# Query transposes moved to a block's end, a prologue with its own PSUM layout, and early steps shifted, in a pooled attention followed by a maxout FFN

The kernel runs on one core of one Trainium2 chip. The metric is the device time of that core in microseconds (us), lower is better. "Span" is the time from the first to the last instruction of the one execution that was profiled; it is about 1.8 us shorter than the measured time of that execution (231.8 beside 233.62 for the kernel before).

## What is computed

```python
# q, k, v: (8 batches, 8 heads, 576 tokens, 64)
k_p = k.reshape(B, H, 72, 8, 64).mean(axis=3)          # keys and values pooled by 8
v_p = v.reshape(B, H, 72, 8, 64).mean(axis=3)
attn = softmax(q @ k_p.T / 8)
x = (attn @ v_p) as 4608 tokens x 512                  # heads side by side
h = max(x @ w1, x @ w2, x @ w3)                        # 512 -> 768
out = h @ w_out                                        # 768 -> 512
```

The kernel uses h = x·w1 + max(0, x·(w2−w1), x·(w3−w1)). The product w1·w_out is made once (`linear`, result `wm`), so only two of the three wide products are done per token.

## The kernel before

Work goes in nine blocks of 512 tokens. Each block has "hidden" parts (x times a weight, then relu and maximum) and "project" parts (the output). A plan says which attention steps of the next batch are slipped in ahead of which part: `k` turns the pooled keys, `T` transposes the queries by DMA, `q` does that on TensorE, `s` makes scores, `v` values, `x` transposes an attention chunk into xT, `d` subtracts w1 from a third of w2 and w3, `w` transposes a piece of w1. A capital `K`, `Q` or `X` is the same step done or copied on VectorE. The number in a pair is the batch.

```python
pools = [stage.enter_context(tc.tile_pool(name="psp", bufs=1, space=PSUM))]
ATT, SC, TR, PW = ("att", 2), ("sc", 2), ("tr", 1), ("pw", 3)   # PSUM tags, buffers

def load_q(b):                                   # GpSimd issues the loads
    qbs[b] = ld.tile([128, 4, NG, D], BF16, name="qb", tag="qb")    # ld: two buffers
    ...
def sub_w(i):
    part = slice(256 * i, 256 * i + 256)
    for t in w_sb[1:]:
        nc.vector.tensor_tensor(out=t[:, :, part], in0=t[:, :, part],
                                in1=w_sb[0][:, :, part], op=ALU.subtract)
...
# ---- end of the prologue, batch 0 (psc: two buffers of two banks) ----
scores2(0)
xn0 = [values(0, c0) for c0, _ in CHUNKS[:2]]
heat(1)                                          # a warming matmul
turn_x(0, 0, 0, xn0[0], PW)
scores2(2)
turn_w(0, nc.scalar.copy)
turn_x(0, 128, 0, xn0[1], PW, nc.vector.tensor_copy)
sub_w(0)
scores2(4)
turn_w(1, nc.vector.tensor_copy)
scores2(6)
nc.vector.memset(kz_all[1], 0.0)

block(0, {0: [(0, "v2")], 1: [(0, "v3 d1")], 2: [(0, "x2")], 3: [(0, "x3 w2")],
          4: [(0, "v4")], 6: [(0, "x4")], 8: [(0, "w3")], 9: [(0, "d2")], ...
          32: [(1, "v1 x0")], 33: [(1, "X1 v2")]}, (hidden, project))

def plan1():                                     # block 1
    return {0: [(1, "v3")], 1: [(1, "x2")], ..., 6: [(2, "k")], 8: [(2, "q0")],
            9: [(2, "q1")], ..., 24: [(2, "x4")], 17: [(2, "s6"), (3, "T")]}

def plan(n):                                     # blocks 2 to 4
    b = n + 1
    ...
    got[1] = [(b + 1, "T")]

# pool_work(n, mm), in words: at the start of block n, all on GpSimd:
#   load k, v, q of batch n + 3, in this order, if there is one,
#   then fold the keys and values of the batches that FOLDS_OF names
```

Chunks of batches 3 and up are also transposed into xT by DMA, from the same queue (SP) as the output stores.

The softmax here doesn't subtract the row's maximum and nothing guards it: scores larger than these inputs give would overflow.

Of the kernel before, what the change touches and what calls it, by code (L numbers as in the profile page):

```python
# [14 lines left out]
def kernel(  # L15
# [11 lines left out]
    nc = tc.nc  # L27
# [3 lines left out]
    B, H, S, D = q.shape  # L31
# [16 lines left out]
    NB = 512  # L48
# [8 lines left out]
    ctx.enter_context(stage)  # L57
    pools = [stage.enter_context(tc.tile_pool(name="psp", bufs=1, space=PSUM))]

# [123 lines left out]
    def turn_k(b):  # L183
        pkt = keys(b, ATT if len(pools) == 1 else SC)
        for par, evac in enumerate((nc.vector.tensor_copy, nc.scalar.copy)):
            fill_kz(b, par, 0, H, pkt, evac if b > 2 else nc.vector.tensor_copy)
# [50 lines left out]
    def values(b, c0):  # L237
        tag = ATT if len(pools) == 1 else ("val", 1)
        pav = psum([128, 2, 512], F32, name="pav", tag=tag[0], bufs=tag[1])
        for h in range(H):  # L240
            nc.tensor.matmul(  # L241
                pav[:, h // 4, 65 * (h % 4):65 * (h % 4) + 65],
                ets[b][:, h, c0:c0 + 128], vp_all[:, b, h, :],
                start=True, stop=True)
        pv = pav[:, :, 0:260].rearrange("p g (h e) -> p g h e", e=65)
        rcp = sb3.tile([128, 2, 4], F32, name="rcp", tag="rcp")
        nc.vector.reciprocal(out=rcp, in_=pv[:, :, :, 64])  # L247
        xn = sb3.tile([128, 2, 4, D], F16, name="xn", tag="xn", bufs=6)
        nc.vector.tensor_tensor(  # L249
            out=xn, in0=pv[:, :, :, 0:D],  # L250
            in1=rcp.to_broadcast([128, 2, 4, D]), op=ALU.mult)
        return xn

    CHUNKS = ((0, 0), (128, 0), (256, 0), (384, 0), (448, 64))
    ATT = ("att", 2)
    SC = ("sc", 2)
    TR = ("tr", 1)
# [5 lines left out]
    def do(b, steps):  # L263
# [3 lines left out]
        for name in steps.split():  # L267
# [4 lines left out]
            elif name[0] == "T":  # L272
                qTs[b] = sb2.tile([128, 2 * NG, 128], BF16, name="qT", tag="qT")
                nc.sync.dma_start_transpose(
                    out=qTs[b], in_=qbs[b].rearrange("p hp t d -> p (hp t d)"))
            elif name[0] == "k":
                turn_k(b)
            elif name[0] == "K":
                fold_k(b, nc.vector)
            elif name[0] == "p":  # L280
                pool_v(b, 4 * i, 4 * i + 4, TR, nc.scalar.copy)
            elif name[0] == "s":
                if i == 0:
                    new_et(b)
                (scores if len(pools) == 1 else scores_flat)(b, i)
            elif name[0] == "d":
                sub_w(i)
            elif name[0] == "w":
                turn_w(i, nc.scalar.copy if i % 2 else nc.vector.tensor_copy)
            elif name[0] == "v":  # L290
                xns[b, i] = values(b, CHUNKS[i][0])
            else:
                turn_x(b, *CHUNKS[i], xns[b, i], ATT if len(pools) == 1 else SC,
                       nc.vector.tensor_copy if name[0] == "X" else nc.scalar.copy)
# [3 lines left out]

    def sub_w(i):

        part = slice(256 * i, 256 * i + 256)
        for t in w_sb[1:]:
            nc.vector.tensor_tensor(out=t[:, :, part], in0=t[:, :, part],  # L303
# [43 lines left out]
    def hidden(n):  # L347
# [3 lines left out]
        if halves:  # L351
            for c0 in (0, NB // 2):
                for jc in range(3):
                    yield from hidden_part(n, jc, c0, c0 + NB // 2, hT)
        for jc in range(3 if halves else 0, JCH):
# [4 lines left out]
    def project(n):  # L360
        hT = hTs[n]
        for mm in range(4):
# [3 lines left out]
            for c in ((slice(0, C // 2), slice(C // 2, C)) if last else (slice(0, C),)):  # L366
                tag = PW if len(pools) == 1 else (PO, SC, PA)[max(0, m - (TOK // 128 - 7))]
                po = psum([128, c.stop - c.start], F32, name="po", tag=tag[0], bufs=tag[1])
# [18 lines left out]

    wm = psum([128, 512], F32, name="wm", tag="tr", bufs=1)

# [6 lines left out]
    k16 = const.tile([96, 6, 4, D], F16, name="k16", tag="k16")  # L396
    pkp0 = psum([128, 6, D], F32, name="pkp", tag="pw", bufs=3)
    heat(10)
# [22 lines left out]
    put_k0(4, 6)  # L421
    turn_q(0, 0, 5, nc.vector.tensor_copy, PW)
    turn_q(0, 5, 9, nc.scalar.copy, ATT)
    pkt0 = [keys(0, PW) for _ in range(2)]
    for h in (0, 4):
# [3 lines left out]
    def scores4(h):  # L429
        psc = psum([128, 4, 256], F32, name="psc4", tag="att", bufs=2)  # L430
        for i in range(4):
# [3 lines left out]
    def scores2(h):  # L435
        psc = psum([128, 2, 512], F32, name="psc2", tag="att", bufs=2)
        for i in range(2):
# [4 lines left out]
    scores4(0)  # L442
    turn_q(0, 9, 14, nc.vector.tensor_copy, PW)
    turn_q(0, 14, 18, nc.vector.tensor_copy, PW)
    pool_v(0, 0, 4, PW, nc.vector.tensor_copy)
    scores4(4)
    pool_v(0, 4, 6, PW, nc.vector.tensor_copy)
    pool_v(0, 6, 8, PW, nc.vector.tensor_copy)
    scores2(0)
    xn0 = [values(0, c0) for c0, _ in CHUNKS[:2]]  # L450
    heat(1)
    turn_x(0, 0, 0, xn0[0], PW)
    scores2(2)
    turn_w(0, nc.scalar.copy)
    turn_x(0, 128, 0, xn0[1], PW, nc.vector.tensor_copy)
    sub_w(0)
    scores2(4)
    turn_w(1, nc.vector.tensor_copy)
    scores2(6)


    nc.vector.memset(kz_all[1], 0.0)
    xns[0, 0], xns[0, 1] = xn0

    FOLDS = (3, 4, 5, 6, 7, 8, 9, 11)

    def block(n, plan, parts, folds=()):

        for slot, _ in enumerate(part for stage in parts for part in stage(n)):
# [5 lines left out]
            if folds and slot in FOLDS:  # L475
                next(folds.pop(0))

    fold_v(1)
    block(0, {0: [(0, "v2")], 1: [(0, "v3 d1")], 2: [(0, "x2")],
              3: [(0, "x3 w2")], 4: [(0, "v4")], 6: [(0, "x4")],  # L480
              8: [(0, "w3")], 9: [(0, "d2")], 12: [(0, "w4")], 13: [(0, "w5")],
              17: [(1, "K")], 24: [(1, "q0 k")], 25: [(1, "q1")],
              26: [(1, "s0 q2")], 27: [(1, "s1 s2")], 28: [(1, "s3 Q3")],
              29: [(1, "s4 s5")], 30: [(1, "s6 s7")], 31: [(1, "v0")],
              32: [(1, "v1 x0")], 33: [(1, "X1 v2")]}, (hidden, project))
    load_k(3, nc.gpsimd)
# [6 lines left out]
    def plan1():  # L493
        return {0: [(1, "v3")], 1: [(1, "x2")], 2: [(1, "v4")], 3: [(1, "x3")],
                5: [(1, "x4")],
                6: [(2, "k")], 8: [(2, "q0")], 9: [(2, "q1")], 11: [(2, "q2 s0")],
                12: [(2, "s1 q3")], 13: [(2, "s2")], 14: [(2, "s3")], 15: [(2, "s4")],
                16: [(2, "s5")], 18: [(2, "s7")],
                19: [(2, "v0")],
                20: [(2, "v1 x0")], 21: [(2, "v2 x1")], 22: [(2, "v3 x2")],  # L500
                23: [(2, "v4 x3")], 24: [(2, "x4")], 17: [(2, "s6"), (3, "T")]}

    def plan(n):
# [3 lines left out]
        got.update({12 + c: [(b, f"v{c} x{c}")] for c in range(5)})  # L507
        got[1] = [(b + 1, "T")]
        return got
# [3 lines left out]
    def pool_work(n, mm):  # L513
# [5 lines left out]
        for name in FOLDS_OF.get(n, "").split():  # L519
# [11 lines left out]

    LEAD = {0: [(6, "s0")], 1: [(6, "s1"), (7, "T")], 2: [(6, "s2")], 3: [(6, "s3")],
            4: [(6, "s4")], 5: [(6, "s5")], 6: [(6, "s6")], 7: [(6, "s7")],
# [277 lines left out]
```

## Time and profile before

| | kernel before |
|---|---|
| three timed runs | 233.75, 235.48, 238.98 us (median 235.48) |
| profiled execution | 233.62 us, span 231.8, granted TensorE clock 0.997 |
| TensorE busy | 221.3 us, 95% |
| VectorE, ScalarE, GpSimd busy | 55%, 52%, 60% |

The page and the chain that the prediction shows carry most of the argument: TensorE is 90% busy or more in every slice from the fifth (23.2 us on) to the 39th. (The prediction says from the sixth; the row that it shows has its first 9 one slice earlier.) Two views more are needed. The first is VectorE's timeline in the prologue; the columns are start, duration, engine, line, operation, out<-in, and in brackets the idle time ahead with what ended it.

```profile
17.55 1.28 DVE L303 TENSOR_TENSOR mw<-mw,mw 128x1024 f16<-128x1024 f16 x2
...
19.33 0.91 DVE L462 MEMSET kz<- 128x1024 uint32 x1 [0.16 <-issue]
```

Both stand ahead of the normalisation of chunk 2, for which TensorE waits. The second is one line of GpSimd's timeline, the load of queries 4:

```profile
71.74 0.78 POOL L92 DMA_DIRECT2D qb<-in_q_dram  x1 [7.16 <-DMA qT<-qb]
```

GpSimd stood still for 7.16 us until a transpose of queries had landed. The prediction names this line in its fourth rival and dismisses it. It turns out to matter.

### The profile page before, as it was taken

The page shows a single profiled execution, that of the slowest core. Times are in us where ns is not written, and L with a number is a line of the kernel's source. Part 1 is how long each engine was busy: PE and PEld are TensorE (multiplying, and loading weights), DVE is VectorE, ACT ScalarE, POOL GpSimd, SP SyncE. Part 2 cuts the span into 40 slices and gives each one's busy share as a digit, 9 for nine tenths or more (in the row PEclk, how much of TensorE's full clock was granted, in tenths as well). Part 3 has the DMA queues.
Part 4 walks back from the last instruction along what each step waited for, and adds up shares of the span by engine and source line. Part 5 has one row for each costly group of instructions (what it writes and reads, how often), then busy time and mean ns, then how long its engine had stood idle before and what let it go on. Part 6 is the DMA issues. An engine that isn't in the chain of part 4 may idle for free.

```text
span 231.8 us, 4548 instructions
## 1 busy us (share of the span) xinstructions
PE 221.3 (95%) x1767; PEld 136.8 (59%) x1767; DVE 128.2 (55%) x237; ACT 120.3 (52%) x215; POOL 138.0 (60%) x113
## 2 busy tenths in 40 slices
PE   7787999999999999999999999999999999999993
PEld 3475745557656455545554555455677666786682
DVE  3659756037334342624262426358779887798730
ACT  2356434755774577227723772385586535465330
POOL 7665202999916999999995999910143442920020
PEclk9999999999999999999999999999999999999998
DMA  6999999999499869978999899973331438211236
GB/s 183 205 198 194 217 197 213 171 185 225 76 202 163 166 162 147 178 172 198 145 179 178 142 206 166 167 158 73 71 71 33 105 71 110 66 27 43 65 76 181
DMA packets 47173, 33.53 MB, mean 145 GB/s; under 512 B 27312, under 2 KB 41904, under 8 KB 47152
## 3 DMA queue, kind: packets, MB, share of 16 engines
q0 software_dynamic: 16960, 16.98, 45.8%
q1 hardware_dynamic: 30032, 16.13, 35.0%
q8 instruction: 14, 0.23, 0.4%
q10 hardware_dynamic: 160, 0.13, 0.2%
q14 instruction: 7, 0.06, 0.1%
HBM read 34.60 MB, written 9.44 MB: 190 GB/s over the span
## 4 chain that ended last, share of the span: by engine, by line
PE 89%; DVE 4%; DMA 2%; ACT 2%; issue 1%; SPq 0%; DVEq 0%
PE pw L330 26%; PE po L374 18%; PE po L370 12%; PE pA L701 7%; PE psc L192 6%; PE pav L241 4%; PE pC L701 3%; PE pm L317 2%; DMA ktTrue<-in_k_dram 2%; PE oA L638 2%; PE pxt L231 2%; PE pB L701 2%; PE pkt L174 1%; ACT et L197 1%; PE pqt L167 1%; DVE mw L303 1%
## 5 line engine op out<-in xcount | busy, mean ns | idle before, releaser
L330 PE MATMUL pw<-xT,mw 128*128 128x512 f16 (+1 forms) x336 | 73.1, 349 | 0.6 <-DVE xT L235 0.3
L338 DVE TENSOR_TENSOR hT<-t,pw 128x512 f16<-128x512 f16 (+1 forms) x42 | 25.5, 610 | 39.7 <-ACT et L197 27.0
L374 PE MATMUL po<-mwo,hT 128*128 128x512 f16 (+1 forms) x198 | 46.8, 372 | 0.0
L330 PEld LDWEIGHTS <-mw 128*128 128x128 f16 x336 | 28.7, 98 | 19.9 <-issue 1.3
L379 ACT COPY osb<-po 128x512 f32<-128x512 f32 (+1 forms) x32 | 18.5, 579 | 42.0 <-PE po L374 36.8
L197 ACT ACTIVATE et<-psc 72x576 f16<-72x576 f32 (+2 forms) x54 | 35.3, 660 | 6.6 <-PE psc L192 6.4
L136 POOL TENSOR_TENSOR half<-vt 72x2048 f32<-72x2048 f16 x7 | 28.4, 4063 | 14.1 <-DMA vt<-in_v_dram 13.7
L370 PE MATMUL po<-wm,xT 128*128 128x512 f16 (+1 forms) x132 | 33.0, 373 | 0.0
L336 ACT ACTIVATE t<-pw 128x512 f16<-128x512 f32 (+1 forms) x42 | 22.5, 536 | 15.9 <-PE pw L330 14.2
L249 DVE TENSOR_TENSOR xn<-pav,rcp 128x512 f16<-128x512 f32 x40 | 27.7, 691 | 1.4
L374 PEld LDWEIGHTS <-hT 128*128 128x128 f16 x198 | 18.4, 98 | 16.2
L137 POOL TENSOR_TENSOR half<-half 72x1024 f32<-72x1024 f32 (+1 forms) x13 | 27.3, 2097 | 1.0
L192 PEld LDWEIGHTS <-kz 128*128 128x128 bf16 x191 | 17.5, 98 | 13.7 <-DVE kz L179 0.4
L192 PE MATMUL psc<-qT,kz 128*128 128x320 bf16 (+2 forms) x168 | 22.4, 246 | 0.4 <-DVE kz L179 0.3
L241 PEld LDWEIGHTS <-et 72*128 72x128 f16 x320 | 15.4, 98 | 8.4 <-issue 0.5
L707 ACT CAST pad<-pA 128x512 f16<-128x512 f32 x27 | 15.3, 587 | 8.4 <-PE pA L701 6.0
L136 POOL TENSOR_TENSOR half<-ktFalse 96x1536 f32<-96x1536 f16 x6 | 18.6, 3099 | 0.3
L247 DVE RECIPROCAL rcp<-pav 128x8 f32<-128x8 f32 x40 | 8.2, 204 | 17.9 <-PE pav L241 17.6
L241 PE MATMUL pav<-vp,et 72*128 72x65 f16 x320 | 17.1, 194 | 0.6 <-ACT et L197 0.6
L370 PEld LDWEIGHTS <-xT 128*128 128x128 f16 x132 | 11.8, 98 | 9.0
L682 DVE SCALAR_TENSOR_TENSOR hT<-pad 128x512 f16<-128x512 f16 x18 | 14.4, 810 | 1.8 <-ACT pad L711 1.4
L701 PEld LDWEIGHTS <-sw 128*128 128x128 f16 x144 | 13.7, 98 | 2.7
(102 smaller groups left out, 274.2 us busy)
## 6 DMA issues: line engine op xcount, KB each, us to landing
out_dram<-osb SPq DMA_DIRECT2D x62, 128.0 KB, 2.8
ktFalse<-in_k_dram POOLq DMA_DIRECT2D x7, 576.0 KB, 7.8
qb<-in_q_dram POOLq DMA_DIRECT2D x7, 576.0 KB, 14.1
vt<-in_v_dram POOLq DMA_DIRECT2D x7, 576.0 KB, 11.6
mw<-in_moe_w_dram POOLq DMA_DIRECT2D x9, 256.0 KB, 9.8
ktTrue<-in_k_dram SPq DMA_DIRECT2D x3, 384.0 KB, 4.8
mwo<-in_moe_w_out_dram POOLq DMA_DIRECT2D x1, 768.0 KB, 12.9
qb<-in_q_dram POOLq DMA_DIRECT2D x2, 288.0 KB, 7.6
```

Of the source, the lines that this page charges most:

```text
L136: e.tensor_tensor(out=f, in0=t[:, :, 0:4, :], in1=t[:, :, 4:8, :], op=ALU.add)
L137: e.tensor_tensor(out=f[:, :, 0:2, :], in0=f[:, :, 0:2, :], in1=f[:, :, 2:4, :], op=ALU.add)
L192: nc.tensor.matmul(out, kz_all[b % 2][:, f % 2, h, :], qTs[b][:, n + i0:n + i1, 64 * (h % 2):64 * (h % 2) + 64], start=True, stop=True)
L197: nc.scalar.activation(out=out, in_=in_, func=FT.Exp, scale=1.0 / 64.0)
L241: nc.tensor.matmul(pav[:, h // 4, 65 * (h % 4):65 * (h % 4) + 65], ets[b][:, h, c0:c0 + 128], vp_all[:, b, h, :], start=True, stop=True)
L249: nc.vector.tensor_tensor(out=xn, in0=pv[:, :, :, 0:D], in1=rcp.to_broadcast([128, 2, 4, D]), op=ALU.mult)
L330: mm = nc.tensor.matmul(pw, w_sb[wi][:, kc, bass.ts(jc, 128)], xT[:, kc, col], start=(kc == 0), stop=(kc == KCH - 1))
L336: nc.scalar.activation(out=t, in_=pw, func=FT.Relu)
L338: nc.vector.tensor_tensor(out=hT[:, jc, c0:c1], in0=t, in1=pw, op=ALU.max)
L370: nc.tensor.matmul(po, xT[:, kc, bass.ts(m, 128)], wm_sb[:, kc, c], start=(kc == 0), stop=False)
L374: nc.tensor.matmul(po, hT[:, jc, bass.ts(mm, 128)], wo_sb[:, jc, c], start=False, stop=(jc == JCH - 1))
L701: mm = nc.tensor.matmul(p[:, w], a[:, kc, bass.ts(g, 128)], b[:, kc, :], start=(i in FIRST and w + kc == 0), stop=(w + kc == 2), skip_grou ...
```

## The change

Its intent: a denser prologue (a third score buffer, cut weight subtractions, the zeroing of the second key buffer out of the way), no stall at the boundary of blocks 0 and 1, and query transposes issued at the end of a block, not in the middle of the next block's loads. The diff, cut to its core:

```diff
-    pools = [stage.enter_context(tc.tile_pool(name="psp", ...))]
+    first = ExitStack()
+    stage.enter_context(first)
+    pools = [first.enter_context(tc.tile_pool(name="ps0", ...))]
+    ATT0, ONE = ("att", 3), ("one", 2)                     # psc4, psc2: bufs 2 -> 3
-                turn_x(b, *CHUNKS[i], xns[b, i], ATT if len(pools) == 1 else SC, ...
+                turn_x(b, *CHUNKS[i], xns[b, i], TR if b == 1 else ATT, ...
-    def sub_w(i):
+    def sub_w(i, j0=0, j1=2, wi=(1, 2)):                   # a half, of chosen weights
...
     scores2(0)
-    xn0 = [values(0, c0) for c0, _ in CHUNKS[:2]]
-    heat(1)
-    turn_x(0, 0, 0, xn0[0], PW)
+    xn0 = [values(0, CHUNKS[0][0])]
     scores2(2)
+    xn0.append(values(0, CHUNKS[1][0]))
+    turn_x(0, 0, 0, xn0[0], ONE)
+    scores2(4)
+    sub_w(0, 0, 1, (1,))
+    turn_x(0, 128, 0, xn0[1], ONE, nc.vector.tensor_copy)
+    sub_w(0, 0, 1, (2,))
+    sub_w(0, 1, 2)
+    scores2(6)
+    first.close()
+    pools.append(stage.enter_context(tc.tile_pool(name="psp", ..., reuse_waits="tile")))
     turn_w(0, nc.scalar.copy)
-    turn_x(0, 128, 0, xn0[1], PW, nc.vector.tensor_copy)
-    sub_w(0)
-    scores2(4)
-    turn_w(1, nc.vector.tensor_copy)
-    scores2(6)
-    nc.vector.memset(kz_all[1], 0.0)
...
+    # hidden halves of block 0 in the order 00 00 01 01 10 10 11 11 02 02 12 12
-    block(0, {0: [(0, "v2")], 1: [(0, "v3 d1")], 2: [(0, "x2")], 3: [(0, "x3 w2")],
-              4: [(0, "v4")], 6: [(0, "x4")], 8: [(0, "w3")], 9: [(0, "d2")], ...
-              33: [(1, "X1 v2")]}
+    block(0, {0: [(0, "v2")], 1: [(0, "v3")], 3: [(0, "x2 x3 w1 v4")], 6: [(0, "x4 d1")],
+              9: [(0, "w2")], 10: [(0, "d2")], ..., 14: [(0, "w5 z")],      # z: the zeroing
+              33: [(1, "X1 v2 v3")]}
     def plan1():
-        return {0: [(1, "v3")], 1: ..., 8: [(2, "q0")], ..., 24: [(2, "x4")], ...
+        return {1: ..., 7: [(2, "q0")], ..., 24: [(2, "x4"), (4, "T")], ...
     def plan(n):
-        got[1] = [(b + 1, "T")]
+        got[18] = [(b + 2, "T")]
-    LEAD = {..., 1: [(6, "s1"), (7, "T")], ...
+    LEAD = {..., 1: [(6, "s1")], ...
```

Some weight folds late in the kernel also come one part earlier; nothing in the traces shows an effect of that.

## The prediction

> **What bounds the kernel now.** I read the page first, then the waits of TensorE, then the chain of waits in order of time, then the timelines of TensorE and GpSimd. All times are us from the span's start.
>
> The page says which engine has nothing to spare and where it has:
>
> ```profile
> span 231.8 us, 4548 instructions
> PE 221.3 (95%) x1767; PEld 136.8 (59%) x1767; DVE 128.2 (55%) x237; ACT 120.3 (52%) x215; POOL 138.0 (60%) x113
> PE   7787999999999999999999999999999999999993
> DVE  3659756037334342624262426358779887798730
> ```
>
> A slice is 5.8 us. TensorE is full from slice 6 to slice 39. Only the first five slices (0 to 29 us) and the last one have gaps, and slice 4 (17.4 to 23.2) is the one in which VectorE is at 9. The diff touches no part of the last slice. In steady state nothing but fewer matmuls could help, and the change removes one matmul in all (a warming one). So the gain has to come from before 60 us. The waits of TensorE name the places:
>
> ```profile
> PE pxt L231 <- DVE xn L249: 0.9, 3, 0.4
> PE pwt L309 <- ACT w1T L310: 0.6, 1, 0.6
> PE pqt L167 <- ACT qT L169: 0.3, 1, 0.3
> PE pw L330 <- DVE xT L235: 0.3, 1, 0.3
> ```
>
> The first two lie in the prologue, the last two at 59.5 and 52.6. These idle times understate the loss, because matmuls waiting one by one count as busy. The chain shows the loss better (start, duration, what):
>
> ```profile
> 17.55 1.28 DVE mw L303 x2
> 18.83 0.34 DVE w1T L310
> 19.16 0.16 issue
> 19.33 0.91 DVE kz L462
> 20.24 0.07 DVE rcp L247
> 20.31 0.02 issue
> 20.34 0.70 DVE xn L249
> ...
> 22.11 1.28 DVE mw L303 x2
> 23.40 0.33 DVE hT L338
> ...
> 24.96 0.40 PE pxt L231 x4
> ...
> 33.39 4.53 PE pm L317 x21
> ```
>
> From 17.5 to 25 the end is set by VectorE: two weight subtractions, the zeroing of the second key buffer, a reciprocal and a normalisation, in its program order. From 24.96 on it is TensorE alone until about 45.
>
> **What the Trainium skill says.** "TensorE: Matmul & The Clock Gate", section "Wait — 56ns, not 53.3ns?": warm matmuls start N / 2.4 GHz + about 2.5 ns apart, 215.7 ns for 512 columns. The chain agrees: 4.53 us for 21 is 216 ns. I therefore count 0.86 us for four matmuls of 512 columns, 0.43 for four of 256, 0.22 for four transposes, 0.26 for a chunk of values. The same page, section "Part 2: What happens when you issue a matmul": only weight loads are pulled ahead, matmuls keep program order. So a step placed too early blocks everything behind it; the waits above fit. "PSUM — Partial Sum Buffer", section "Specifications (TRN2)": eight banks per partition. Three score buffers of two banks plus two single ones fill all eight, hence the separate layout; the trace shows no banks. "DMA: Bandwidth & Descriptors", section "Issuing engines are not separate DMA queues": all queues share the same 16 engines. The trace agrees: the query transpose of batch 6, issued into the loads of batch 7, took 15.3 us to land; the one of batch 4 took 3.9.
>
> **The change part by part.**
>
> Score buffers. Before, the second score pair (heads 2, 3) waits for a buffer and its exp starts at 16.84; the last exp ends at 19.45 (17.89 + 1.56). With three buffers that pair is issued right after the first values (about 14.9). The exps of 0.70 us then end at about 16.0, 17.5 and 18.25, with one 0.58 us copy between. So the last one is done 1.2 us earlier.
>
> VectorE in the prologue, in its new order. The second normalisation ends at 16.75 as before. The first piece of a weight (half of a 0.64 to 0.68 us subtraction, about 0.42 with its fixed part) may start, since that weight landed at 16.1: to 17.18. Copy of the second transposed chunk, 0.42: to 17.62 (17.63 before). Three more pieces (the third weight landed at 17.4): to 18.89. Chunk 2: reciprocal 0.21, normalisation 0.69: to 19.8, where before it was 21.04. A maximum 0.41, then chunk 3: to 21.1, before 22.20. The 0.91 zeroing and the second pair of subtractions, 1.28, are gone from here.
>
> TensorE behind it. The first hidden part starts at about 17.9 (18.56 before). Chunks 2 and 3 are transposed at 20.1 and 21.1, chunk 3 is copied by ScalarE to 21.9, and the fifth part, the first that needs it, runs at 21.9. Chunk 4 is transposed by 23.45; before it was 25.36 (24.96 + 0.40), 1.9 later. Of the 1.9, a weight transpose that before had been done by then comes back (0.22). The second pair of subtractions, now started at 23.3, holds the parts that need it by about 0.3. What remains is **1.4 us** when the last hidden part of the block ends (33.39 before, about 32.0 then). The rest to 45 is TensorE work at peak and only moves. No landing stops this: the output weight landed at 29.25, keys 1 at 32.5 and queries 1 at 35.3; they are needed at 32.0, 34.5 and 36.5. Their landings are set by a queue that is full from 4 us on.
>
> Block boundary. Moving chunk 3 of batch 1 (0.26) ahead of the block fills the wait of 0.26 for the copy at 52.6: **0.26**. The queries' first turn one step earlier lets its copy end before the second turn: the wait of **0.34** at 59.5 goes. The single transpose buffer for batch 1 is no loss: its copies of 0.58 fit between turns 0.87 apart.
>
> Query transposes. They move three steps, about 3.5 us, from the next block's loads to the calm before them. They should land in 4 to 6 us instead of up to 15.3. But the queries are used a block later, so this is worth **0**.
>
> Sum: 1.4 + 0.26 + 0.34 = 2.0 us.
>
> **What caps it.** GpSimd folds keys and values in one chain, which starts when the values of batch 1 land (39.2) and nothing in the change moves that. Its ends and the TensorE steps that need them:
>
> ```profile
> 45.86 1.27 POOL L139 TENSOR_TENSOR vp<-half 72x512 f16<-72x512 f32 x1
> 48.71 0.42 PE L241 MATMUL pav<-vp,et 72*128 72x65 f16 x8
> ...
> 54.32 0.99 POOL L139 TENSOR_TENSOR kp<-half 96x384 bf16<-96x384 f32 x1
> 57.04 0.44 PE L174 MATMUL pkt<-ident,kp 96*64 96x96 bf16 x6
> ```
>
> ```profile
> 77.61 0.99 POOL L139 TENSOR_TENSOR kp<-half 96x384 bf16<-96x384 f32 x1
> 80.56 0.44 PE L174 MATMUL pkt<-ident,kp 96*64 96x96 bf16 x6
> ```
>
> The slack is 48.71 - 47.13 = 1.58, then 57.04 - 55.31 = 1.73, then 80.56 - 78.60 = 1.96 us. TensorE arrives there 1.4, 1.66 and 2.0 earlier. So the sum just fits, and any more would turn into a wait for GpSimd. I take **1.9 us**: the span goes to about 229.9.
>
> **The rivals.** (1) *The prologue gives much less*: the pieces cost more than half each, or the new layout's first buffers wait for the old ones' last readers. For it: VectorE is full there and the third weight lands at 17.4, so the start barely moves. Against: 0.91 and 1.28 us really leave the chain. Then 0.5 + 0.6 = 1 us. (2) *The prologue gives more*, up to the 3 us or so that TensorE still loses in 14 to 25. Against: the three slacks above. Even then 2 us remain, with a new wait for the folds at about 79; only an earlier GpSimd chain would pass that. (3) *New waits eat the gain*: a query transpose at a block's end waits for its load (batch 4's landed at 83.4, after that block's end) and holds the output stores queued behind it; or the single buffer stalls. Against: five output buffers, and the next store is due a dozen steps later. This would cost 0.5 to 1 and leave 1 us. (4) *The collision of transposes and loads matters more than I think*, because it delays loads and folds. For it: GpSimd idles 7.2 us before 71.74, marked as released by a query transpose. But that one, batch 3's, keeps its place, and later folds have 5 us or more to spare.
>
> **Range and chances.** The run that was profiled took 233.62 us for a span of 231.8. The three timed runs were 233.75, 235.48 and 238.98, so the scatter of one kernel is larger than the gain. A good run should take 233.7 - 1.9 = 231.8; with a scatter like that before, the median of a few lies about 1 us higher: 232.8. The range is 230.4 (a gain of 3.3 in a quiet run) to 235.4 (no gain, or a noisy median). Faster by over 2% needs 4.7 us, more than the slacks allow, and could come only from the scatter: 0.09. Within 2%: 0.89. Slower: 0.02.
>
> **What would show it right or wrong.** Right: the chain no longer holds the zeroing in 17 to 25; the first product of the weights starts at about 32.0 (33.23 before), the first values of batch 1 at 47.3, its neighbours as above; no wait of TensorE at the boundary and at the second query turn; transposes landing in 4 to 6 us with TensorE unmoved by it; keys of batch 3 turned at 78.6 to 78.8, right behind GpSimd. From there to the end both traces should run in parallel, about 1.9 apart. Wrong: TensorE waits of over 0.5 us between 23 and 60, or a longer last slice, or a distance that still grows after 80 us, which would mean that steady state held waits I took for work.

## The result

| | before | after |
|---|---|---|
| timed runs | 233.75 to 239.53, median 236.91 (six) | 231.37 to 235.83, median 231.64 (six) |
| profiled span | 231.8 | 230.2 |
| TensorE busy | 221.3 us (95%) | 220.2 us (96%) |

The ratio of the fast runs is 0.988, with a 95% interval of 0.984 to 0.992: within 2%. (A ratio here is the mean time of one kernel's fast runs over that of the other's fast runs of the same rounds, so it isn't quite the ratio of the medians quoted. A run more than 1.5% above the fastest of its kernel counts as slow and is left out of verdicts.)

The page of the kernel after, in the lines that answer to those in the prediction:

```profile
PE 220.2 (96%) x1766; PEld 137.1 (60%) x1766; DVE 128.2 (56%) x238; ACT 120.9 (53%) x216; POOL 137.9 (60%) x113
...
PE   7688999999999999999999999999999999999992
...
DVE  3558867037425333633362336278579887897730
```

The first 9 of TensorE's row is in the fifth slice, as before; in the four slices ahead of it 7, 7, 8, 7 have become 7, 6, 8, 8. VectorE's 9 in slice 4 has become an 8. TensorE's waits after the change all lie in the prologue; these three bear on the argument (waited for, us in total, times, longest):

```profile
PE pvp L158 <- DMA vt<-in_v_dram: 0.8, 1, 0.8
PE pxt L233 <- DVE xn L251: 0.6, 2, 0.4
...
PE pw L335 <- ACT xT L237: 0.2, 1, 0.2
```

The two waits of 0.3 at the boundary are gone. The wait for the values of batch 0 is new: in this execution the first loads landed later than in the one profiled before. The chain shows that the second pair of subtractions now bites:

```profile
22.18 0.59 ACT xT L237
...
24.29 0.70 DVE mw L308
...
25.04 1.21 PE pw L335 x8
```

To see where the gain arises, I read the same TensorE steps in both traces:

| step of TensorE | before | after | gain inside the stretch |
|---|---|---|---|
| first pooled values of batch 0 | 11.89 | 12.67 | −0.78 |
| first product w1·w_out | 33.23 | 33.03 | +0.98 |
| keys 3 turned (in block 2) | 80.56 | 79.55 | +0.81 |
| keys 4 turned (in block 3) | 103.68 | 102.31 | +0.36 |
| keys 5 turned (in block 4) | 126.73 | 125.08 | +0.28 |
| end of span | 231.8 | 230.2 | −0.05 |

The sum is 1.6. The first row isn't shown to be the change's doing: in all 14 traces these values start 0.14 to 0.18 us after the first load of batch 0's values has landed, and that load is issued at 3.9 us in each. It landed so that they start at 11.6 to 12.1 in the four traces with the old prologue and at 12.0 to 12.8 in the ten with the new one; what sets its landing was not tested. The second stretch, on the other hand, repeats. It measures 21.34 us in all four traces of schedules with the old prologue (before, e2, e7, e9), and 20.35 to 20.40 in the five traces with the new one uncut (after, e1, e3, e5, e6).

The predicted sizes were 1.4 for that stretch, 0.6 for the boundary, 0 for the query transposes, capped at 1.9 by the folds. The total is about right, but two of its parts are not, and the folds have moved in a way I had excluded. GpSimd's timeline after the change:

```profile
70.11 0.78 POOL L94 DMA_DIRECT2D qb<-in_q_dram  x1 [5.45 <-DMA qT<-qb]
...
75.97 0.99 POOL L141 TENSOR_TENSOR kp<-half 96x384 bf16<-96x384 f32 x1
```

and TensorE's turn of these keys:

```profile
79.55 0.44 PE L176 MATMUL pkt<-ident,kp 96*64 96x96 bf16 x6
```

The fold of keys 3 ends at 76.96, 1.64 earlier than before, although values 1 (the chain's start) came no earlier. TensorE turns those keys at 79.55, with 2.59 to spare. So my cap was never reached, and GpSimd's chain is not a fixed clock: it hangs on the landing of the transpose of queries 3, which took 8.8 us from its issue before and 7.3 after.

### The profile page after: what moved, and what is told of

Same layout as the page of the kernel before. It is cut to its first block, busy times and chain, and to the rows that moved or that the text cites. A ratio compares the mean times of both kernels' runs of the same rounds, so it can differ in the third digit from the quotient of the medians.

```text
span 230.2 us, 4549 instructions
## 1 busy us (share of the span) xinstructions
PE 220.2 (96%) x1766; PEld 137.1 (60%) x1766; DVE 128.2 (56%) x238; ACT 120.9 (53%) x216; POOL 137.9 (60%) x113
## 4 chain that ended last, share of the span: by engine, by line
PE 89%; DMA 4%; DVE 2%; issue 1%; ACT 1%; POOL 1%; POOLq 0%; DVEq 0%
PE pw L335 27%; PE po L384 18%; PE po L380 12%; PE pA L712 7%; PE psc L194 5%; PE pav L243 4%; DMA vt<-in_v_dram 4%; PE pC L712 3%; PE pm L322 2%; PE oA L649 2%; PE pB L712 2%; PE pxt L233 1%; PE pkt L176 1%; DVE xn L251 1%; PE oC L649 1%
## 5 line engine op out<-in xcount | busy, mean ns | idle before, releaser
L341 ACT ACTIVATE t<-pw 128x512 f16<-128x512 f32 (+1 forms) x42 | 22.6, 537 | 14.8 <-PE pw L335 13.1
L693 DVE SCALAR_TENSOR_TENSOR hT<-pad 128x512 f16<-128x512 f16 x18 | 14.4, 810 | 1.8 <-ACT pad L722 1.4
```

Of the source, the lines that this page charges most:

```text
L341: nc.scalar.activation(out=t, in_=pw, func=FT.Relu)
```

## Theories and experiments

Questions after the first comparison:

1. Is the prologue's 0.98 VectorE's order, as I said, or the score buffers? And what holds the missing 0.4?
2. Do the two boundary moves do what I said, and no more?
3. What made blocks 3 and 4 start 0.36 and 0.28 sooner? Theory A: the new place of the query transposes, which leave SP's queue and the DMA engines to the chunk transposes at a block's end. Theory B: the earlier prologue alone. Theory C, formed after the first four runs: the load of queries 4 goes into the buffer of queries 3, so it must wait for the transpose that reads them; that wait holds GpSimd, shifts the next bursts of loads, and the bursts then collide with the chunk transposes at a block's end.

The recorded expectations of e1, e2 and e7 use the letters otherwise: there A is the prediction's "their place is worth 0", and B says that at the old place the transposes run into the loads, which is A here. C is the same.

| run | what it is | fast runs | all runs: median (range) | ratio to before | span |
|---|---|---|---|---|---|
| e1 | after, query transposes back | 6 of 6 | 233.26 (231.41–233.76) | 0.999 [0.994, 1.003] | 232.0 |
| e2 | before, query transposes moved | 3 of 6 | 237.16 (232.75–241.95) | 1.000 [0.997, 1.003] | 231.0 |
| e3 | after, boundary back | 5 of 6 | 233.27 (231.89–243.12) | 0.999 [0.994, 1.004] | 231.2 |
| e4 | after, second pair in pieces | 5 of 6 | 233.23 (232.36–238.22) | 1.000 [0.996, 1.004] | 232.0 |
| e5 | after again | 18 of 19 | 231.85 (231.19–235.54) | 0.990 [0.986, 0.994] | 229.7 |
| e6 | after, own query buffers | 5 of 6 | 231.68 (231.28–235.04) | 0.988 [0.981, 0.995] | 229.6 |
| e7 | before, own query buffers | 22 of 22 | 233.43 (233.01–235.18) | 0.997 [0.994, 1.000] | 231.3 |
| e8 | e4, own query buffers | 15 of 17 | 232.78 (232.00–237.66) | 0.994 [0.991, 0.997] | 231.2 |
| e9 | before again, one look | – | 238.78 (one run, state unknown) | – | 237.0 |
| e10 | e6, second pair apart | 4 of 6 | 231.90 (230.79–237.07) | 0.990 [0.981, 0.999] | 230.4 |
| e11 | after, zeroing back | 6 of 12 | 236.62 (232.29–246.13) | 1.001 [0.997, 1.005] | 231.8 |
| e12 | after, two score buffers | 8 of 20 | 237.28 (232.08–244.14) | 0.995 [0.991, 0.998] | 230.6 |

e1 to e4 ran on one chip, e5 to e8 on a second, e9 to e12 on a third. All gave right results. The ratios come from fast runs alone; the medians do not, and where a kernel's runs fall into two groups they say mostly how many runs fell into the slower one. Effects below 1 us are read from the traces.

### e1: the query transposes at their old place in the kernel after

```diff
-        got[18] = [(b + 2, "T")]
+        got[1] = [(b + 1, "T")]          # and in plan1 and LEAD as before
```

> The changed kernel with only the five query transposes put back to where they were before (one step into the next block). Theory A, that of the prediction: their place is worth 0, so this takes 231.6 us like the changed kernel, within 0.2, and TensorE waits for nothing at the start of blocks 3 and 4 (about 101 and 124 us). Theory B, read from the two traces afterwards: placed there they run into the load burst of keys, values and queries, the burst ends later (queries of batch 6 landed 14.1 us after issue against 11.7), the chunk transposes of the batch land after 4 to 5 us instead of 2.4 to 3.7, and the first product of block 4 (perhaps of block 3 too) waits: 0.3 to 0.65 us more, 231.9 to 232.3, with a gap of 0.2 to 0.4 in TensorE's chain before the first product of block 4.

TensorE's timeline has one pause after the prologue, at the start of block 3:

```profile
103.18 1.02 PE L335 MATMUL pw<-xT,mw 128*128 128x512 f16 x4 [2.23 <-DMA xT<-xn]
```

It waits 2.23 us for a chunk transpose. The kernel before had only 0.2 there. Block 4 starts without a wait: from keys 4 to keys 5 takes 22.75 us, as after the change (22.77), and not 23.05 as before. So with the transposes at the old place block 3 lost more than I saw before, and block 4 lost nothing. The transpose itself isn't what the chunks met in block 3: that of queries 4 had landed at 85.5, before the first load of the next burst went out at 86.7. Something else decides what collides. Here queries 3 landed 8.8 us after their issue and held GpSimd for 7.28 us, as in the kernel before, so the loads of batch 5 went out no earlier than there (86.7 to 88.1), while the shorter prologue had brought the pair of chunk transposes forward to 95.68. This is where theory C comes from. The time, 233.26, sits near the kernel before, but five of the six runs lie between 231.96 and 233.76, so I take no size from it.

### e2: the query transposes moved in the kernel before

```diff
-        got[1] = [(b + 1, "T")]
+        got[18] = [(b + 2, "T")]         # and in plan1 and LEAD as after
```

> The kernel before with only the query transposes moved to the end of the block before. Theory A: equal to the kernel before (0.0). Theory B: the gap of 0.28 us at the start of block 4 (125.65 to 125.77 and the slow first product after it) closes, and perhaps that of 0.35 at the start of block 3: 0.3 to 0.6 us faster than before. The prologue stays as it was: the first product of the weights starts at about 33.2.

The profile shows no TensorE wait after 60 us. Keys 3 to 4 take 22.86 and 4 to 5 take 22.76 us, so the gain at the starts of blocks 3 and 4 is there without the new prologue: theory B falls. The span of 231.0 is 0.8 below that of before. The ratio of 1.000 rests on three fast runs and doesn't resolve this. Three of six runs took 240.7 to 242.0, so the new place alone does not keep the kernel out of its slower group.

### e3: the boundary steps at their old place in the kernel after

```diff
-              33: [(1, "X1 v2 v3")]}        +              33: [(1, "X1 v2")]}
-        return {1: [(1, "x2")], ... 7: [(2, "q0")]
+        return {0: [(1, "v3")], 1: [(1, "x2")], ... 8: [(2, "q0")]
-  TR if b == 1 else ATT                     +  ATT
```

> The changed kernel with the block boundary put back: chunk 3 of batch 1 after the boundary, the first query turn one step later, chunk transposes of batch 1 in the score buffers. By the prediction this gives back 0.26 + 0.34 = 0.6 us (232.2), shown as a wait of about 0.26 for the copy before the first product of block 1 and of about 0.34 for the copy before the second query turn. The rival: GpSimd's chain holds TensorE later anyway (keys of batch 3), then nothing is lost; in the changed kernel's trace that slack is 2.5 us, so I expect the loss.

The waits of TensorE from 33 to 60 us are exactly those of the kernel before (the kernel after has none there):

```profile
PE pqt L169 <- ACT qT L171: 0.3, 1, 0.3
PE pw L335 <- DVE xT L237: 0.3, 1, 0.3
```

From the first product w1·w_out to keys 3 it takes 47.32 us, against 46.52 after and 47.33 before. So the two moves are worth 0.80 together, 0.2 more than the two waits that the profile names; they were not taken back singly. The parts of this change are separable here: e3 keeps the 20.36 of the prologue.

### e4: the second pair of subtractions in pieces

```diff
-  3: [(0, "x2 x3 w1 v4")], 6: [(0, "x4 d1")], 9: [(0, "w2")]
+  3: [(0, "x2 x3 w1 e0 v4")], 4: [(0, "e1")], 6: [(0, "x4")], 7: [(0, "e2")], 9: [(0, "w2")]
   # e0: a half for w2, e1: the same half for w3, e2: the other halves of both
```

> The changed kernel with the second pair of weight subtractions cut up too: the two halves that the parts of the eighth step need are put into VectorE's idle stretches at about 22.0 (0.65 idle) and 23.6 (0.36 idle), the rest one step after the last place. Theory: in the changed kernel TensorE loses about 0.6 us from 24.3 to 26.3 (12 products take 1.90 where 1.30 is peak) to these subtractions, a term that I sized at 0.3; then this is 0.5 to 0.6 us faster, 231.0, and the first product of the weights starts at about 32.4 instead of 33.0. Rival: the stretch is bound by the landing of the weights (second parts landed at about 20 and 21.5) or by the normalisations, then it is equal to the changed kernel.

The stretch shrinks from 20.36 to 20.03. The twelve products behind the transposes of chunk 4 show it. From the start of that group to the next transposes took 1.74 us after the change (24.34 to 26.08) and takes 1.31 here, which is their 12 × 0.108 us at peak:

```profile
23.94 1.47 PE L337 MATMUL pw<-xT,mw 128*128 128x256 f16 x12
25.25 0.39 PE L316 MATMUL pwt<-identh,mw 128*128 128x128 f16 x4
```

So the late pair held TensorE for 0.44 us, of which 0.33 reach the end of the stretch. But the kernel isn't faster, for it loses more later. Keys 4 to 5 take 23.17 in place of 22.77 (a collision of block 4, see e7), and at 161 us there is a new wait,

```profile
PE po L382 <- DVE hT L345: 0.8, 1, 0.8
```

and the part behind keys 7 takes 71.57 us, where after the change it takes 69.87. Nothing in that part was edited. The first output product there starts at 161.64, right behind VectorE's reading of the newest hidden part; after the change it starts at 160.71, before the reading of the same part ends (161.48). So it seems to go into another of the PSUM buffers. Why it does is not shown: e4 adds no PSUM tile, and e11, which adds no instruction and only moves one, has the same wait. e8 repeats the loss with other landings, so it comes with this instruction order and isn't chance.

### e5 and e6: the kernel after again, and with query buffers of its own for even and odd batches

```diff
-        qbs[b] = ld.tile([128, 4, NG, D], BF16, name="qb", tag="qb")
+        qbs[b] = ld.tile([128, 4, NG, D], BF16, name="qb", tag=f"qb{b % 2}", bufs=1)
-          "S4": ld.tile([128, 9, HALF], F16, name="so4", tag="qb")}
+          "S4": ld.tile([128, 9, HALF], F16, name="so4", tag="qb0", bufs=1)}
```

The order of the instructions is the same on every engine and the space is the same. Only which buffer a load goes into changes: queries 4 now go where queries 2 were, which TensorE turned long ago.

> The changed kernel itself, unaltered, so that the other runs of this call have it on the same chip. Its first profile had 231.9 us; the four runs of the first call scattered within the fast state between 231.4 and 234.2. Theory C: the scatter has one cause, the landing of the query transpose of batch 3 (8.8 us after issue in two traces, 7.3 in another), on which the load of queries 4 and with it GpSimd's whole chain waits; then this kernel's runs fall into a group near 231.5 and one near 233.5, and its profile belongs to the slower group exactly if that transpose took 8 us or more and the first product of block 3 waited for a chunk transpose.

> The changed kernel with the query loads of odd and even batches in buffers of their own; the order on every engine is unchanged. In the changed kernel queries 4 are loaded into the buffer of queries 3 and wait for their transpose: GpSimd stands idle 5.5 us (7.2 in the kernel before). With own buffers they wait only for TensorE's last turn of queries 2 (about 61.5). Theory C: GpSimd's idle time goes, keys of batch 3 are folded by about 72 instead of 77, the load burst of batch 5 starts at about 80 (held then only by TensorE's first product of block 2) instead of 84.8, is over before the chunk transposes of batch 3 at 93 to 98, and these land within 3 us: no wait at the start of blocks 3 and 4, runs near 231.5 without a slower group. If theory C is wrong (chunk transposes slow for another reason), the times scatter as the changed kernel's do.

e5 repeats the result: 0.990, with 13 of 19 runs between 231.19 and 232.13; five of the others lie between 232.91 and 233.96, about where the second group was expected, but none of these was profiled. In its trace queries 3 landed after 6.7 us and held GpSimd for 4.7; TensorE has no wait after 60 us. In e6 queries 4 are issued at 64.62 with no pause before, and keys 3 are folded at 71.48, 5.48 earlier than in the first trace after the change. TensorE then has the same pace (keys 3 to 5 at 78.98, 101.75, 124.51, where e5 has 79.06, 101.83, 124.59), and the times are equal: 231.68 and 231.85. So the gate through the shared buffer exists, and in executions like these removing it buys nothing, as TensorE does not wait for GpSimd anyway. The expectation of no slower group wasn't met in full: one of e6's six runs took 235.04.

### e7: the kernel before with the same two buffers

> The kernel before with the same own query buffers and nothing else. Theory C: its two waits at the start of blocks 3 and 4 (0.35 and 0.28 us) are the same thing and go, 0.6 us faster than before in the trace, although the query transposes stay where they were. If the place of the transposes is what matters (theory B), the wait at block 4 stays.

This is the run that separates the place of the transposes from the gate. The place is the old one, and queries 3 landed later than in any other trace, 19.0 us after their issue. The lines: SP's issue of that transpose, then GpSimd's load and the fold of keys 3.

```profile
62.49 9.77 SPq L274 DMA_TRANSPOSE qT<-qb  x1
```

```profile
63.98 0.79 POOL L92 DMA_DIRECT2D qb<-in_q_dram  x1
...
69.86 0.99 POOL L139 TENSOR_TENSOR kp<-half 96x384 bf16<-96x384 f32 x1
```

GpSimd no longer waits, and the late landing harms nobody: the first scores of batch 3 come at 82.83, just after it. Keys 3 to 4 and 4 to 5 take 22.77 and 22.76 us, as after the change. So the 0.64 of blocks 3 and 4 can be had without moving a transpose.

For block 3 the other traces agree. The table has, per trace, when GpSimd issued the load of queries 5 (the end of a burst), when SP issued the pair of chunk transposes that block 3 needs, the time between them, how long after that issue the load landed, when behind the load the first of the pair landed, and the time from keys 3 to keys 4:

| trace | load | chunks | between | load lands after | pair behind load | keys 3 to 4 |
|---|---|---|---|---|---|---|
| e1 | 88.14 | 95.68 | 7.5 | 5.6 | 1.61 | 25.16 |
| e11 | 87.15 | 96.34 | 9.2 | 3.7 | 1.63 | 23.52 |
| before | 87.86 | 97.26 | 9.4 | 3.3 | 1.64 | 23.12 |
| e9 (clock dips, see there) | 93.63 | 102.82 | 9.2 | 3.1 | 1.64 | 24.58 |
| e2 | 87.61 | 96.97 | 9.4 | 3.0 | 1.63 | 22.86 |
| e4 | 85.95 | 95.55 | 9.6 | 2.5 | 1.66 | 22.77 |
| after | 86.21 | 96.26 | 10.1 | 2.1 | 1.66 | 22.76 |
| e3 | 86.83 | 97.22 | 10.4 | 2.1 | 1.67 | 22.77 |
| e10 | 81.60 | 96.53 | 14.9 | 1.5 | 2.06 | 22.77 |
| e8 | 80.71 | 95.49 | 14.8 | 1.4 | 2.94 | 22.77 |
| e5 | 85.19 | 95.77 | 10.6 | 1.4 | 1.77 | 22.77 |
| e7 | 82.49 | 97.42 | 14.9 | 1.2 | 2.49 | 22.77 |
| e12 | 85.44 | 96.29 | 10.9 | 1.0 | 1.67 | 22.77 |
| e6 | 80.75 | 95.91 | 15.2 | −1.2 | 3.69 | 22.77 |

In the eight traces at the top, where the load lands 2 us or more after the pair went out, the first of the pair lands 1.61 to 1.67 us behind the load, whenever that is. Up to 2.5 us of overlap block 3 has time to spare; from 3.0 on its first product comes late, and the loss grows with the overlap. The first product of block 3, before and in e11:

```profile
102.73 1.02 PE L330 MATMUL pw<-xT,mw 128*128 128x512 f16 x4 [0.20 <-issue]
```

```profile
102.19 1.02 PE L335 MATMUL pw<-xT,mw 128*128 128x512 f16 x4 [0.59 <-DMA xT<-xn]
```

(The profile calls the first wait "issue", but the second of the pair had landed at 102.64, 0.09 before, the same distance as in e11.) That is theory C, and no trace needs theory A beside it: e11 has the moved transposes and loses 0.75, e7 has the old place and loses nothing, and e2 and before lie in the order of their overlaps. Block 4 shows the same. The load of queries 6 landed 3.7 us (before) and 3.9 us (e4) after the pair of chunk transposes went out, and these two alone lost time there, 0.28 and 0.40; in the other twelve it landed 2.1 us after or sooner. Why that load took 14.0 us in these two and 10.7 to 13.5 in the other traces with the shared buffers remains open.

As to the times: all 22 runs were fast (233.01 to 235.18), while in the same call 40 of 51 runs of the kernel before were slow and reached 245.26.

e7 also gives the cleanest comparison of spans, since neither it nor e5 loses anything in blocks 3 and 4: 231.3 against 229.7. That is 1.6 us for prologue and boundary. By stretches it is 0.99 + 0.80 − 0.14 for a later start = 1.65.

### e8: the pieces of e4 with the buffers of e6

> The changed kernel with the second subtractions in pieces (which started the first product of the weights at 32.30 instead of 33.03, 0.6 earlier against the first product of the values) and own query buffers. If the prologue's 0.6 us were lost only at blocks 3 to 5 through late chunk transposes, this keeps them: 0.5 to 0.6 us faster than own buffers alone, about 231.0, a candidate better than both. If something later takes it back, equal to own buffers alone.

The stretch is 20.03 again, and so are the wait of 0.8 at 161 us and a longer end. At 232.78 it stays behind e5 and e6 of the same call.

### e9: the kernel before, one more look

I wanted a profile of the slower group of the kernel before, and this one caught it: 238.78 us. A single run has no state, so it gives no verdict on speed. It shows a mechanism, in one execution.

> The kernel before, unaltered, for one more profile. In the second call 40 of its 51 runs were over 236.5 us (state slow), but none of the 22 runs of the kernel before with own query buffers. If the profile falls in that group, I expect the same path as in the other traces, only longer: the transpose of queries 3 lands late, queries 4 are issued late, keys of batch 3 are folded after TensorE needs them (about 80.6), and waits for chunk transposes follow at blocks 3 to 5. If it falls in the fast group, it should repeat the first profile: first product of the weights 21.3 us after the first product of the values, waits of about 0.2 at the start of blocks 3 and 4.

The longest wait of TensorE, and the chain from 62 to 85 us:

```profile
PE pkt L174 <- POOL kp L139: 3.7, 1, 3.7
```

```profile
62.57 14.40 DMA qT<-qb
...
77.54 0.77 POOL qb L92
...
78.33 3.10 POOL half L136
...
83.39 1.00 POOL kp L139
84.43 0.44 PE pkt L174 x6
```

Queries 3 landed 14.4 us after their issue, where the first trace had 8.8. GpSimd, stopped at the load of queries 4, began the fold of keys 3 5.8 us later, and TensorE waited 3.66 us for these keys. In the first trace the same TensorE step had 1.96 to spare. This pause costs more than itself. The page's row of the granted clock:

```profile
PEclk9999999999999979999999999999999999999998
```

A 7 in the slice right behind the pause (83 to 89 us): eight products of 512 columns take 2.96 us there, 1.90 in the first trace. The Trainium skill, "TensorE: Matmul & The Clock Gate", section "What's actually happening", says that the array falls to half its clock after an idle window of about 3.4 us, until it has been busy for as long; a pause of 3.66 with slow products behind it agrees. Turning keys 3 comes 3.87 later than in the first trace, keys 3 to 4 take 24.58 in place of 23.12 (1.46 more), and together that is 5.3, beside a span that is 5.2 longer. The 14 traces show what goes with a late landing: the lead of this transpose over the first load of the next burst (keys 4), which GpSimd issues as soon as it has folded values 2, while the transpose goes out when queries 3 have landed. With a lead of 0.82 to 1.12 us (six traces) the transpose landed after 6.7 to 7.3 us, with 0.53 to 0.78 (six more) after 8.5 to 9.8, with 0.31 (e9) after 14.4 and with 0.09 (e7, where the load of queries 4 goes out in the same burst) after 19.0. This is read from the traces and not tested: no run set the lead on purpose.

### e10: the second pair of subtractions apart but whole, with own buffers

```diff
-  3: [(0, "x2 x3 w1 v4")], 6: [(0, "x4 d1")]
+  3: [(0, "x2 x3 w1 e0 v4")], 4: [(0, "e1")], 6: [(0, "x4")]     # e0: w2 whole, e1: w3 whole
```

> The changed kernel with own query buffers, and with the two instructions of the second pair of subtractions kept whole but apart, in VectorE's two idle stretches (before and after the normalisation of chunk 4). Theory: TensorE's loss at 24.3 to 26.3 is these subtractions, so the stretch from the first product of the values to the first product of the weights shrinks from 20.36 to 19.9 or 20.0, as with the pieces (20.03), and since no instruction is added the buffers of the later blocks come out as in the changed kernel, so that the gain is kept to the end: 231.2, 0.4 faster than own buffers alone. If the end again falls to 232.5, the later loss of the pieces (a wait of 0.8 for VectorE at about 161 and 0.7 at the end) comes with any earlier place of the subtractions and not with the number of instructions.

Inconclusive. In the profiled execution the granted clock dipped in the third slice, and TensorE waited 2.0 us for the first key sums, so its stretch of 20.89 can't be compared. The end is kept, without the 0.8 wait of e4. The lowest run of the whole study, 230.79, is one of its four fast ones, but its mean doesn't stand out from e5 or e6 (ratios 0.990, 0.990, 0.988).

### e11: the zeroing back ahead of block 0

```diff
-  14: [(0, "w5 z")]                          +  14: [(0, "w5")]
+    nc.vector.memset(kz_all[1], 0.0)         # behind the prologue's last scores
```

> The changed kernel with the zeroing of the second key buffer (0.91 us on VectorE) put back ahead of block 0. By the prediction's reading VectorE's order sets the end there, so the stretch from the first product of the values to the first product of the weights should grow from 20.36 by 0.9, to about 21.2, nearly all of the 0.98 that the changed kernel gained in it. Rival: only the score buffers matter, then it stays near 20.4.

The stretch grows from 20.36 to 21.12, by 0.76 of the 0.91 that the zeroing takes, so VectorE's order does set the end here. A later loss rides along as in e4 (a wait of 0.8 for hT, and 0.6 for a chunk transpose), which is why the span of 231.8 overstates it.

### e12: two score buffers

```diff
-    ATT0, ONE = ("att", 3), ("one", 2)       # psc4, psc2: bufs=3
+    ATT0, ONE = ("att", 2), ("one", 2)       # psc4, psc2: bufs=2
```

> The changed kernel with two score buffers instead of three in the prologue. By the prediction the three buffers end the last exp 1.2 us earlier, but VectorE's second normalisation, copy and subtractions end at the same time either way, so the stretch from the first product of the values to the first product of the weights should stay within 0.3 of 20.36. Rival: the buffers are what gains, then it grows to 21 or more.

The stretch grows to 20.97, by 0.61. I had taken the third buffer to be nearly worthless for the end as long as VectorE is the bound; that was wrong. Two new waits of TensorE show what it buys:

```profile
PE pqt L169 <- DVE qT L171: 0.6, 1, 0.6
PE psc L194 <- ACT et L199: 0.4, 1, 0.4
```

A turn of queries now waits 0.6 for a copy to free its buffer, and a score pair 0.4 for an exp, so that values and normalisations start later on VectorE. Note that 0.76 (e11) and 0.61 (e12) add up to more than the whole 0.98: each was taken back with the other in place, so they can't be summed. The new order of the hidden halves, the pieces of the first subtractions and the moved weight transposes were not taken back, so their share isn't shown.

Both e11 and e12 keep the query transposes at the new place and the shared buffers, and half or more of their runs were slow (up to 246.13 and 244.14). So the slower group isn't a mark of the kernel before alone.

## Why the prediction was right or wrong

**Time and class: right.** 231.64 lies in the range of 230.4 to 235.4, 1.2 below the figure. The difference is in the allowance for scatter: I expected the median about 1 us above a good run, and here five of six runs lay within 0.55 of each other. The good run itself, put at 231.8, came at 231.37 to 231.92. The span fell by 1.6 in the first pair of traces; I had said 1.9. That these are so close is luck in part: the prologue gave 0.4 less than I said, the boundary 0.2 more, blocks 3 and 4 gave 0.64 where I had 0, and the start was 0.78 later.

**The bound and the place of the gain: right.** TensorE at 95% in steady state could give little, and most of the gain lies before 80 us, but not all, as said below. The neighbour steps named in advance (zeroing gone from the chain, no wait at the boundary) are as described, and e11 confirms that VectorE's order sets the end of the stretch.

**Prologue, 1.4: right mechanism, term too large.** It measured 0.98, so the first product w1·w_out came at 33.03 and not at about 32.0, or at 32.25 if the later start is taken off. I had put all of it on VectorE's order; e12 shows that 0.61 of it is lost again without the third score buffer. Reckoned from the first pooled values, the transposes of chunk 4 came 1.62 earlier, not 1.9; 0.2 of that gap is a wait of TensorE for ScalarE's copy of chunk 3, which I had counted as hidden. Behind them I took off 0.22 for the weight transpose that comes back, which was so, and 0.3 for the second pair of subtractions, which was 0.44 (e4). That gives 1.62 − 0.22 − 0.42 = 0.98, with 0.42 the loss beyond peak in that part of the trace.

**Boundary, 0.26 + 0.34 = 0.60: right, a little small.** Taking both moves back costs 0.80 (e3).

**Query transposes, 0: the value stands as far as the runs show, the reasoning behind it is the failed step.** I wrote that they should land sooner but that "the queries are used a block later, so this is worth 0". No run shows their place to be worth anything: e7 loses nothing in blocks 3 and 4 with the old place, e11 loses 0.75 with the new one. But I missed two things. First, the queries' own use isn't the only thing that waits for the landing: the load of the next batch's queries waits for it through the shared buffer, and with it the fold of keys 3 and the next burst of loads. Second, that burst's timing decides whether the chunk transposes at the end of the block come in time. Before, the pair issued from 97.26 on landed after 4.9 and 3.7 us and block 3's first products were held up; after, they took 3.7 and 2.8. My fourth rival had this line in hand and set it aside because "that one, batch 3's, keeps its place, and later folds have 5 us or more to spare". But the fold right behind it had only 1.96, and the landing isn't a constant: 6.7 to 19.0 us over these traces. So one of the prediction's own signs of being wrong came true, "a distance that still grows after 80 us": the two traces lie 1.01 apart at keys 3 and 1.65 at keys 5. These 0.64 are not shown to be the change's doing, for the transpose of queries 3 keeps its place, and with the change in it the kernel can lose them again (e11).

**They "should land in 4 to 6 us": right for three of the four that were moved.** After the change those of batches 4 to 7 took 4.0, 4.0, 14.2 and 4.2; batch 6's still ran into loads. (Batch 3's, 7.3, keeps its place. The expectation of e1 speaks of five that were put back; its edit moves four.)

**The cap by the folds: wrong.** "Nothing in the change moves that" was true of the chain's start, not of its middle. Keys 3 were folded at 76.96, not about 78.6, and TensorE turned them 2.6 us after that, not right behind. The same step had the opposite error as well: in e9 the fold ended 5.8 us later and TensorE waited. A slack read from one trace isn't a property of the kernel when a DMA landing stands in the chain.

**What the slow runs are.** I took the scatter of the kernel before as noise of the chip. e9 shows, in one execution, a path by which the kernel itself makes 5 us of it, and e7's 22 fast runs of 22, beside 11 of 51, fit the removal of that path. That every slow run has this cause isn't shown: e6, e8 and e10, with own buffers, still had one, two and two slow runs, none of them profiled, and e5, with the shared buffers, had 18 of 19 fast in the same call as e7.

**A faster version.** None was found beyond doubt. The kernel after with own query buffers (e6) is as fast as the kernel after, and it removes a dependency on a landing; six runs are too few to call it steadier.

## What to carry to other kernels

When a queue of an in-order engine holds both loads and work, look up which earlier reader each load's buffer must wait for: a buffer rotation that hands a load the tile of a slow DMA reader puts that DMA's landing into the chain of everything behind it. A slack is only as good as the spread of the landings in it, so read it in several executions, with and without the slow ones, before you use it as a cap. And after cutting one engine's early work, follow the landmarks to the very end: e4 and e8 won 0.33 us early and lost more in a part that nobody had edited.

## What the Trainium skill lacked or had wrong

- "DMA: Bandwidth & Descriptors" (section "Latency and other measured facts") gives an effective 261 GB/s for a DMA transpose. The query transposes here move 128 × 2304 elements of two bytes, 590 KB, in 3.9 us at best, which is 151 GB/s from issue to landing, and in 6.7 to 19.0 us beside loads, 88 to 31 GB/s. (These times hold whatever fixed part a transfer has, so the two are not quite the same measure.) The page gives no figure for a transpose that shares the engines with loads; here a chunk transpose issued into a burst landed 1.61 to 1.67 us behind the burst's last load, which made 3.7 to 7.2 us from its issue.
- The same page has nothing on how long the issue of such a transpose holds its queue when the engines are full: SP was held 1.9 to 2.1 us in most traces for the transpose of queries 3, 7.46 in e9 and 9.77 in e7, and 5.7 to 11.3 for other ones that met a burst of loads.
- No page warns that a buffer rotation can make a load wait for a DMA transpose of an earlier batch, with everything behind it on GpSimd: 4.7 to 13.25 us of idle GpSimd in the traces with the shared buffers, none with own ones.
